# Front steps over one channel block of two tiles (4096 elements an instruction) in a fused VQ codec kernel, with engine queues found anew

## The chip, the cores and the metric

The kernel runs on one core of one Trainium2 chip. The metric is the device time of one execution in microseconds (us). Five engines of the core work side by side: TensorE (PE: matrix products, with PEld for its weight loads), VectorE (DVE), ScalarE (ACT), GpSimd (POOL) and SyncE (SP), which here does nothing but issue DMAs. Each engine works through its own queue in order.

## The reference, cut to what matters

```python
xp = pad(x, 1 row on both sides)            # x (2, 16000, 512) bf16
z = sum(xp[:, i:i+T, :] * dw_enc[i] for i in range(3))   # per-channel taps
z = silu(z)
res, q = z, 0
for s in range(4):                           # residual quantisation, codebooks (4, 8, 512)
    d2 = |res|^2 - 2 res.cb[s] + |cb[s]|^2
    sel = cb[s][d2.argmin(-1)]
    q, res = q + sel, res - sel
y = sum(qp[:, i:i+T, :] * dw_dec[i] for i in range(3))   # qp: q padded
```

So each of the 32,000 tokens is filtered along time by a three-tap filter with one weight per channel and tap, gated, assigned a code word in each of four stages, and the sum of the four chosen code words is filtered again.

## The kernel before, in words

**Tiles.** The tokens are cut into 18 tiles of G rows of 128 tokens, 9 for each batch row: G = 8, 10, 12, 16 six times | 16 six times, 12, 10, 8. Tiles 3 to 14 have G = 16, that is 2048 tokens. A tile's data lie in SBUF with channels on the partitions, four channel blocks of 128 (i = 0 to 3), in the ring buffer XR (in the code XT is its view): for each block G + 2 slots of 128 tokens, the two more for the edges. XR has 108 slots, six tiles of 18. Loading tile n + 6 therefore has to wait until tile n's residual has been read for the last time, by the grams of its fourth stage.

**Steps of a tile**, with the keys that the code gives them:
- load: SP issues one transposing DMA for each slot (L631), and one for an edge slot (L643, L649) where the neighbour is another tile. Tiles 0 and 1 are loaded otherwise (L601, transposed on PE and copied at L622).
- front, for one piece of the tile: three taps, each a product with a per-partition scalar, into TA, EX and in place into XR (L681 on ACT, L682 on DVE), two additions on DVE (L402), exp of the negative on ACT (L689), plus 1 (L691). front2: reciprocal on ACT (L700) and the gate, a product on DVE (L402). The helper `either` lets a tap, a copy or a cast run on ACT or on DVE.
- select: the grams of the first stage on PE (score0, L719), a chain of short DVE instructions (decide, L754 to L859) with transposes on PE between, by which the codes of the first three stages are chosen.
- resid: PE forms the residual behind three stages (L914, L919), ACT or DVE casts it into XR (L941, L942). score3 (L719 again) and decide (L956 on) choose the last code.
- windows and back: the one-hot codes are laid out (L878, L884, L885) and the decoder's products are made on PE (L997), cast into one of four buffers YB (L1006 on ACT, L1007 on DVE) and stored by SP (L1034).

**Pieces.** In a tile of G = 16 a piece is two channel blocks, nb = 2: exp, plus 1, reciprocal, gate and additions handle 2 x 2048 = 4096 elements per partition. A tap can't, since its scalar differs from channel block to channel block: each piece has six taps of 2048 elements. There are 36 pieces, put into groups (RUNS) of 2, 3, 3, then 4, at the end 2; the exps of a group follow each other under one table load, and so do its reciprocals. NE = 4 buffers EX hold the pieces of a group. EARLY = 2 is the number of tiles loaded the other way.

**Order.** The order of every engine's instructions is fixed by hand-written tables: RANK gives a step's place, WHERE the engine (A or D) of each step that has the choice. A planner reads them; at run time nothing but semaphores is left. The fills (L1062) are products without use that fill gaps on PE.

## Time and profile before

| | us |
|---|---|
| time of the runs shown | 579.2 and 581.91, median 580.56 |
| the profiled execution's own time | 584.83 |
| its span | 582.9 |
| DVE busy | 540.3 (93%) |
| ACT busy | 537.5 (92%) |
| PE busy | 463.2 (79%) |
| POOL busy | 80.2 (14%) |

The span is the part of the profiled execution between its first and last instruction; 584.83 − 582.9 = 1.93 us lie around it. Its own time is 584.83 − 580.56 = 4.27 us above the median of the runs. The profile lists for each engine its busy time and instructions, groups them by line, operation and shape with the mean duration of one, and names for each idle stretch what ended it. Durations of neighbouring instructions on DVE and ACT overlap a little, so what an instruction costs in a full queue is read from start to start.

### The profile page before, as it was taken

How to read it: one execution, taken by the hardware profiler on the slowest of the kernel's cores; microseconds unless marked ns; L12 is line 12 of the kernel's file. 1: busy time of each engine (PE TensorE's matmuls, PEld its weight loads, DVE VectorE, ACT ScalarE, POOL GpSimd, SP SyncE). 2: the span in 40 equal slices, each digit the busy share in tenths (PEclk: the TensorE clock that was granted, in tenths of full speed). 3: DMA queues.
4: the chain of work that ended last, by engine and by line, in shares of the span. 5: the costliest groups of instructions: out<-in, count | busy, mean ns of one | idle time of the engine just before them, and what ended most of it. 6: DMA issues, size and time to landing. Idle time of an engine off the chain costs nothing.

```text
span 582.9 us, 27362 instructions
## 1 busy us (share of the span) xinstructions
PE 463.2 (79%) x12366; PEld 226.0 (39%) x12462; DVE 540.3 (93%) x1028; ACT 537.5 (92%) x423; POOL 80.2 (14%) x140
## 2 busy tenths in 40 slices
PE   7855768768786788878886898677888888889994
PEld 4322334433433243443434244333334444445442
DVE  4999999998999899999999999999999999988642
ACT  4898999999999999999999999989999999999563
POOL 6014101002001420012000103202022112000000
PEclk9768879997899799899999899999999989999999
DMA  8444454544574555867767696696695531232354
GB/s 249 97 100 101 94 98 87 92 66 109 87 150 99 118 113 112 198 87 144 130 131 138 120 146 136 130 178 148 114 213 87 174 92 42 75 111 76 133 197 157
DMA packets 153384, 71.81 MB, mean 123 GB/s; under 512 B 144710, under 2 KB 144742, under 8 KB 153012
## 3 DMA queue, kind: packets, MB, share of 16 engines
q1 hardware_dynamic: 153052, 69.64, 56.2%
q8 instruction: 97, 1.59, 1.2%
q10 hardware_dynamic: 216, 0.43, 0.2%
q14 instruction: 19, 0.16, 0.1%
HBM read 2.79 MB, written 32.77 MB: 61 GB/s over the span
## 4 chain that ended last, share of the span: by engine, by line
DVE 31%; ACT 22%; SPq 19%; PE 15%; issue 7%; DMA 3%; DVEq 0%; ACTq 0%
SPq L631 16%; DVE XR L402 8%; ACT XR L941 5%; ACT EX L700 5%; PE banks L914 5%; ACT YB L1006 5%; DVE EX L402 4%; ACT EX L689 3%; PE banks L919 3%; DMA out_dram<-YB 3%; PE banks L719 2%; PE banks L997 2%; DVE TA L682 2%; DVE XR L682 2%; ACT EX L681 2%
## 5 line engine op out<-in xcount | busy, mean ns | idle before, releaser
L402 DVE TENSOR_TENSOR XR<-XR,EX 128x4096 bf16<-128x4096 bf16 (+3 forms) x72 | 145.0, 2020 | 0.3 <-ACT EX L700 0.2
L941 ACT CAST XR<-banks 128x1024 bf16<-128x1024 f32 (+2 forms) x125 | 110.6, 943 | 13.6 <-PE banks L919 13.5
L1006 ACT CAST YB<-banks 128x1024 bf16<-128x1024 f32 x114 | 112.9, 1048 | 9.0 <-DVE OHALL L402 2.5
L689 ACT ACTIVATE EX<-XR 128x4096 bf16<-128x4096 bf16 (+3 forms) x36 | 115.5, 3209 | 4.6 <-DVE XR L402 4.5
L700 ACT ACTIVATE EX<-EX 128x4096 bf16<-128x4096 bf16 (+3 forms) x36 | 115.4, 3212 | 0.1
L719 PE MATMUL banks<-XR 128*32 128x64 bf16 x8064 | 93.1, 201 | 14.0 <-issue 5.6
L719 PEld LDWEIGHTS <-XR 128*32 128x32 bf16 x8064 | 78.3, 98 | 58.9 <-issue 49.7
L802 POOL COPY OHDS<-OHALL 128x256 bf16<-128x256 bf16 (+3 forms) x36 | 48.4, 1344 | 361.0 <-DVE OHALL L402 346.5
L919 PE MATMUL banks<-OHR,WR 32*128 32x512 bf16 (+2 forms) x1152 | 82.9, 358 | 1.3 <-DVE OHR L859 0.7
L402 DVE TENSOR_TENSOR EX<-TA,EX 128x4096 bf16<-128x4096 bf16 (+3 forms) x36 | 72.5, 2014 | 0.0
L914 PE MATMUL banks<-XR,IDENT 64*64 64x512 bf16 (+2 forms) x576 | 56.6, 379 | 11.6 <-ACT XR L941 3.9
L1062 PE MATMUL banks<-MSK,IDENT 128*128 128x512 bf16 x200 | 58.3, 434 | 8.3 <-issue 2.9
L997 PE MATMUL banks<-WDEC,OHW 128*128 128x512 bf16 x145 | 48.6, 392 | 15.3 <-ACT XR L941 4.8
L914 PE MATMUL banks<-XR,UP 64*64 64x512 bf16 (+2 forms) x576 | 55.1, 363 | 1.5 <-issue 1.5
L919 PEld LDWEIGHTS <-WR 32*128 32x128 bf16 x1152 | 24.0, 92 | 61.2 <-issue 55.2
L682 DVE TENSOR_SCALAR TA<-XR,WENC 128x2048 bf16<-128x2048 bf16 (+3 forms) x69 | 47.2, 690 | 0.2
L914 PE MATMUL banks<-XR,DOWN 64*64 64x512 bf16 (+2 forms) x576 | 42.0, 367 | 0.0
L682 DVE TENSOR_SCALAR EX<-XR,WENC 128x2048 bf16<-128x2048 bf16 (+3 forms) x60 | 40.4, 683 | 0.7 <-DMA XR<-in_x_dram 0.6
L691 DVE TENSOR_SCALAR EX<-EX 128x4096 bf16<-128x4096 bf16 (+3 forms) x36 | 39.3, 1100 | 0.0
L682 DVE TENSOR_SCALAR XR<-XR,WENC 128x2048 bf16<-128x2048 bf16 (+3 forms) x57 | 38.4, 678 | 0.0
L1062 PEld LDWEIGHTS <-IDENT 128*128 128x128 bf16 x223 | 22.9, 108 | 34.8 <-issue 17.6
L914 PEld LDWEIGHTS <-IDENT 64*64 64x64 bf16 x576 | 19.8, 106 | 36.1 <-issue 29.1
(138 smaller groups left out, 586.2 us busy)
## 6 DMA issues: line engine op xcount, KB each, us to landing
out_dram<-YB SPq DMA_DIRECT2D x34, 448.0 KB
out_dram<-YB SPq DMA_DIRECT2D x28, 512.0 KB
XR<-in_x_dram SPq DMA_TRANSPOSE x263
out_dram<-YB SPq DMA_DIRECT2D x28, 60.0 KB
XR<-in_x_dram SPq DMA_DIRECT2D x1, 1280.0 KB
XR<-in_x_dram SPq DMA_DIRECT2D x1, 1024.0 KB
out_dram<-YB SPq DMA_DIRECT2D x30, 2.0 KB
out_dram<-YB SPq DMA_DIRECT2D x2, 224.0 KB
```

The lines of the kernel that those rows point to most:

```text
L402: add("DVE", cost, key, lambda: nc.vector.tensor_tensor(out=out, in0=a, in1=b, op=op), reads, writes, **kw)
L631: nc.sync.dma_start_transpose(out=X[:, :, g + 1, :], in_=src[g])
L682: lambda dst=to, src=src, w=w: nc.vector.tensor_scalar(out=dst, in0=src, scalar1=w, scalar2=None, op0=ALU.mult),
L689: add("ACT", act(nb * R), ("exp", n, i0), lambda: nc.scalar.activation(v(ex), Z, ACT.Exp, scale=-1.0), zt, ext + ["ACTTAB"], hold="E")
L700: nc.scalar.add_instruction(mybir.InstActivation(name=nc.get_next_instruction_name(), engine=mybir.EngineType.Activation, func=ACT.Reciprocal,
L719: nc.tensor.matmul(o[HB * q:HB * (q + 1), u * ZW:(u + 1) * ZW].rearrange("p (s c) -> p s c", s=2), lhsT=blk, rhs=both, start=False, stop=( ...
L914: nc.tensor.matmul(at(r)[to], lhsT=dia[h, h], rhs=Z[h, i, r:G:RG, :], start=start, stop=False)
L919: nc.tensor.matmul(at(r), lhsT=WR[v][g, i * P:(i + 1) * P], rhs=W[g, v // 3, 0:rows_of[r], :], start=False, stop=stop)
L941: either({"ACT": act_psum(2 * k * P), "DVE": dve(2 * k * P)}, key(1), lambda dst=dst, src=src: nc.scalar.copy(dst, src()), lambda dst=dst, ...
L997: nc.tensor.matmul(o, lhsT=W[:, k, PADC:PADC + P], rhs=WDEC[u], start=True, stop=not wrap)
L1006: either({"ACT": act_psum(1024), "DVE": dve(1024)}, key, lambda dst=dst, box=box: nc.scalar.copy(dst, ps(box)), lambda dst=dst, box=box: n ...
L1062: nc.tensor.matmul(PS[j // 2][:, 512 * (j % 2):512 * (j % 2) + NMK * ZW], lhsT=IDENT, rhs=MSK.rearrange("p u w -> p (u w)"), start=True, s ...
```

## The change

Ten of the twelve large tiles are taken in pairs, TWINS = (4,5), (6,7), (8,9), (10,11), (12,13). For these a piece is one channel block of both tiles instead of two channel blocks of one. The number of pieces stays 36, their size 4096 elements, and a tap needs one scalar now, so that it is one instruction of 4096 elements, in two runs of 2048 since the tiles lie apart in XR (`rows_from`). A piece of a pair needs both tiles' loads, and either tile's first grams need all four gates of the pair. PAIRS, an unused way of selecting two tiles at once, is taken out. RANK and WHERE are new from end to end.

```diff
+    TWINS = [(4, 5), (6, 7), (8, 9), (10, 11), (12, 13)]
-    PAIRS = ()
-    RANK = ("000304000m02000a0d050f04030109010106050d0d0g0g0q080f06040f0c0i020e0307010G0c130t0E090H0n0r0h0u000I0i10080f0k0o0w0D0O0U04"
...
+    RANK = ("000000000309040b0c01090a07020605010a0e0308020b0f070e0504000701090d0g0F0106070N0g0J0w0S080d0x1b0j0H0r0y0h0l0p0t0E0P0T0U04"
...
-    pieces = [(st, i) for st in tiles for i in range(0, KT, st["nb"])]
+    twin = {a: (tiles[a], tiles[b]) for a, b in TWINS}
+    pieces = []
+    for st in tiles:
+        if st["n"] in twin:
+            pieces += [(twin[st["n"]], i) for i in range(KT)]
+        elif not any(st in t for t in twin.values()):
+            pieces += [(st, i) for i in range(0, KT, st["nb"])]
...
+    def front_twins(sts, i):
+        G = sts[0]["G"]
+        R = G * P
+        lo, hi = sorted(st["xo"] for st in sts)
...
+        def rows_from(k):
+            one = XT[:, i, lo + k:lo + k + G, :]
+            return bass.AP(tensor=one.tensor, offset=one.offset, ap=[one.ap[0], ((hi - lo) * P, 2), (1, R)])
+        both = lambda t: t[:, 0:2 * R].rearrange("p (u x) -> p u x", u=2)
+        Z = rows_from(2)
...
+        for k, dst, tok in ((0, both(TA), [("TA", c) for c in range(KT)]), (1, both(ex), ext), (2, Z, xi)):
+            src, w = rows_from(k), WENC[:, k, i:i + 1]
+            either({"ACT": act(size) + 0.09, "DVE": dve(size, 3.84) + 0.06}, key, lambda dst=dst, src=src, w=w: nc.scalar.mul(dst, src, w),
+                   lambda dst=dst, src=src, w=w: nc.vector.tensor_scalar(out=dst, in0=src, scalar1=w, scalar2=None, op0=ALU.mult),
+                   allx + ["WENC"] + ([] if k == 2 else xi), tok)
```

The changed instruction lists differ in these counts (taps of 1024 to 1536 elements are those of the small tiles; "copies" are OHR, pads and windows from PSUM):

| | before | after |
|---|---|---|
| DVE: all rows | 1030 | 993 |
| DVE: taps of 2048 | 124 | 19 |
| DVE: taps of 4096 | 0 | 49 |
| DVE: casts into XR of 1024 / 768 / 512 | 7 / 7 / 5 | 9 / 6 / 10 |
| DVE: casts into YB | 12 | 15 |
| DVE: copies of OHR 1024 / 768 / 512, of pads 1024 | 6 / 2 / 0, 4 | 10 / 1 / 2, 7 |
| ACT: all rows | 428 | 405 |
| ACT: taps of 2048 | 20 | 5 |
| ACT: taps of 4096 | 0 | 11 |
| ACT: casts into XR of 1024 / 768 / 512 | 89 / 17 / 19 | 87 / 18 / 14 |
| ACT: casts into YB | 114 | 111 |
| ACT: copies of OHR 1024, of pads 1024 | 6, 5 | 2, 2 |
| ACT: table loads | 22 | 22 |
| SP: transposing loads, stores | 263, 132 | 263, 132 |

Where the instructions now stand is seen best at two places. In the lists below, the last number or product is the shape of the output, and a trailing x3 means three in a row.

DVE, the first taps of tile 4, before. EX, TA and XR are the taps' targets, L402 additions and decide steps, L754, L755 and L780 decide steps of earlier tiles:

```order
L691 TENSOR_SCALAR EX3_77<-EX3_77 128x4096
L682 TENSOR_SCALAR EX0_74<-XR_72,WENC_62 128x2048
L682 TENSOR_SCALAR TA_73<-XR_72,WENC_62 128x2048
L402 TENSOR_TENSOR PR_89<-PR_89,TR_92 128x80
L682 TENSOR_SCALAR TA_73<-XR_72,WENC_62 128x2048
L402 TENSOR_TENSOR KEY0_82<-PR_89,CCB_71 128x80
L754 TENSOR_REDUCE E2_91<-banks_99 128x8
L755 TENSOR_TENSOR SC_88<-banks_99,CC2_70 128x192
L780 TENSOR_REDUCE MN_93<-KEY0_82 128x10
```

DVE, the first taps of the pair (4,5), after:

```order
L793 TENSOR_REDUCE E2_91<-banks_99 128x8
L794 TENSOR_TENSOR SC_88<-banks_99,CC2_70 128x192
L689 TENSOR_SCALAR TA_73<-XR_72,WENC_62 128x4096
L689 TENSOR_SCALAR EX0_74<-XR_72,WENC_62 128x4096
L689 TENSOR_SCALAR EX1_75<-XR_72,WENC_62 128x4096
L407 TENSOR_TENSOR EX0_74<-TA_73,EX0_74 128x4096
L689 TENSOR_SCALAR TA_73<-XR_72,WENC_62 128x4096
L793 TENSOR_REDUCE E2_91<-banks_99 128x8
```

Three taps of 2048 with decide steps between have become taps of 4096 elements that stand together; three products of two different pieces follow each other.

SP, the stretch that ends with the last load that the first taps of tile 13 need (the last of the six in the last row), before. L631 are loads, L1034 stores:

```order
L631 DMA_TRANSPOSE XR_72<-in_x_dram 128x4x128 x2
L1034 DMA out_0_dram<-YB0_84 1x1024
L1034 DMA out_0_dram<-YB0_84 112x2048
L1034 DMA out_0_dram<-YB0_84 15x2048
L631 DMA_TRANSPOSE XR_72<-in_x_dram 128x4x128 x4
L1034 DMA out_0_dram<-YB2_86 128x2048
L631 DMA_TRANSPOSE XR_72<-in_x_dram 128x4x128 x6
```

SP, the stretch that ends with the last load that the first taps of the pair (12,13) need (the third of the four in the last row), after. L636 and L654 are loads, L1073 stores:

```order
L1073 DMA out_0_dram<-YB1_85 128x2048
L636 DMA_TRANSPOSE XR_72<-in_x_dram 128x4x128 x3
L654 DMA_TRANSPOSE XR_72<-in_x_dram 128x4x128
L636 DMA_TRANSPOSE XR_72<-in_x_dram 128x4x128 x15
L654 DMA_TRANSPOSE XR_72<-in_x_dram 128x4x128
L636 DMA_TRANSPOSE XR_72<-in_x_dram 128x4x128 x4
L1073 DMA out_0_dram<-YB2_86 128x2048
L636 DMA_TRANSPOSE XR_72<-in_x_dram 128x4x128 x4
```

Before, at most 14 loads stand between two stores once the first store has gone out; here there are 24 in a row ahead of one store. Counted from the start of the list, the pair's last load is the 211th and has 38 stores ahead of it; before, tile 13's last load is the 210th and has 46.

More of the change, by code (lines that the diff above doesn't have):

```diff
@@ L1042 @@
         for st, i in group:
[L1043 to L1045 removed]
+            if i == 0:
+                for u in st if isinstance(st, tuple) else (st,):
+                    if u["n"] >= EARLY:
+                        load(u)
+                        hold(u)
             done.append(front(st, i))
[L1047 to L1048 removed]
+        for d in done:
+            front2(*d)
         for st, i in group:
[L1050 to L1058 removed]
+            if isinstance(st, tuple):
+                ready = st if i + 1 == KT else ()
+            else:
+                ready = (st,) if i + st["nb"] == KT else ()
+            for t in ready:
+                select([t])
+                for sub in range(len(t["subs"])):
+                    resid(t, sub)
+                back(t)
     def fill(j, k):
```

129 lines of the change are left out of this document (66 added, 63 removed).

## The prediction

> **What bounds the kernel now.** I read the page's busy shares first, then the busy time by stretches, then the chain that ended last, then the groups by shape, at last single stretches of the timeline. The page, then the table by stretches (start:end, length, busy time of the engines with their instructions in brackets, granted TensorE clock, DMA share, GB/s):
>
> ```profile
> span 582.9 us, 27362 instructions
> PE 463.2 (79%) x12366; PEld 226.0 (39%) x12462; DVE 540.3 (93%) x1028; ACT 537.5 (92%) x423; POOL 80.2 (14%) x140
> DVE 31%; ACT 22%; SPq 19%; PE 15%; issue 7%; DMA 3%; DVEq 0%; ACTq 0%
> ...
> core 0: us, PE busy (x) PEld busy (x) DVE busy (x) ACT busy (x) POOL busy (x), PEclk, DMA share, GB/s
> 0.00:100.00 100.00, 71.47 (x928) 34.97 (x936) 91.76 (x169) 85.67 (x76) 22.49 (x76) 0.83 0.54 119
> 160.00:225.00 65.00, 51.04 (x1415) 23.74 (x1428) 63.38 (x114) 63.33 (x46) 13.81 (x9) 0.95 0.60 117
> 295.00:360.00 65.00, 53.51 (x1529) 25.30 (x1542) 64.73 (x113) 64.66 (x49) 8.63 (x7) 0.97 0.73 126
> 360.00:460.00 100.00, 80.40 (x2343) 38.09 (x2360) 97.25 (x183) 96.65 (x73) 16.48 (x17) 1.00 0.76 158
> 531.00:583.00 52.00, 42.19 (x1141) 20.68 (x1149) 27.41 (x73) 31.04 (x38) 1.15 (x5) 0.98 0.46 157
> ```
>
> DVE and ACT are both full from 100 us to 531 us: of the 65 us up to 360 DVE leaves 0.27 and ACT 0.34 open. At 531 DVE ends its last gate; after it neither is full, and PE has the most to do (42.2 of 52 us). So the time is: start, the work that DVE and ACT must do up to the last gate, their waits, and a tail of 52 us. DVE's busy time before 531 is 540.3 − 27.4 = 512.9 us, its idle time 531 − 512.9 = 18.1. Two waits at the start make 7.4 of that; 10.7 lie in the middle:
>
> ```profile
> 1.49 0.28 DVE L530 TENSOR_REDUCE SMT<-IDENT 128x4 f32<-128x128 bf16 x1 [1.49 <-POOL IDENT masks.py:199]
> 8.97 1.29 DVE L622 COPY XR<-banks 128x1024 bf16<-128x1024 bf16 x2 [5.91 <-PE banks L612]
> 529.81 1.21 DVE L402 TENSOR_TENSOR XR<-XR,EX 128x2048 bf16<-128x2048 bf16 x1
> ```
>
> A third queue is near its limit, and the chain gives it 19%: SP. Two of its rows (minimum/median/maximum ns, first to last start) and the moment at which tile 13's loads are just in time:
>
> ```profile
> L631 SPq DMA_TRANSPOSE XR<-in_x_dram x234: 1188/1266/2769, 1.7 to 478.7; - x117
> SPq L631 <- PE banks L719: 13.1, 3, 6.3
> 349.57 10.34 SPq L631 DMA_TRANSPOSE XR<-in_x_dram  x6
> 361.83 1.42 DVE L682 TENSOR_SCALAR EX<-XR,WENC 128x2048 bf16<-128x2048 bf16 x2 [0.59 <-DMA XR<-in_x_dram]
> ```
>
> SP issues a load in 1.27 us at the median; the wait for the grams of the fourth stage (13.1 us) is the wait for slots in XR. Tile 13's last load ended its issue at 349.57 + 10.34 = 359.91, and DVE's first tap came 1.92 us later, having waited 0.59.
>
> **The change, part by part.** Prices. The rows by shape (count, busy us, mean ns), then four of the timeline (start, us):
>
> ```profile
> L682 DVE TENSOR_SCALAR TA<-XR,WENC 128x2048 bf16<-128x2048 bf16 x47 | 35.2, 755 | 0.2
> L682 DVE TENSOR_SCALAR XR<-XR,WENC 128x2048 bf16<-128x2048 bf16 x39 | 28.8, 741 | 0.0
> L682 DVE TENSOR_SCALAR EX<-XR,WENC 128x2048 bf16<-128x2048 bf16 x38 | 28.4, 758 | 0.6 <-DMA XR<-in_x_dram 0.6
> L691 DVE TENSOR_SCALAR EX<-EX 128x4096 bf16<-128x4096 bf16 x24 | 29.1, 1225 | 0.0
> L691 DVE TENSOR_SCALAR EX<-EX 128x2048 bf16<-128x2048 bf16 x4 | 2.7, 678 | 0.0
> L402 DVE TENSOR_TENSOR XR<-XR,EX 128x4096 bf16<-128x4096 bf16 x48 | 109.3, 2282 | 0.0
> L402 DVE TENSOR_TENSOR EX<-TA,EX 128x4096 bf16<-128x4096 bf16 x24 | 54.8, 2281 | 0.0
> L1007 DVE CAST YB<-banks 128x1024 bf16<-128x1024 f32 x12 | 14.5, 1220 | 2.0 <-PE banks L997 1.3 <-PE banks L878 0.8
> L942 DVE CAST XR<-banks 128x512 bf16<-128x512 f32 x5 | 3.4, 689 | 2.3 <-PE banks L919 2.3
> L942 DVE CAST XR<-banks 128x1024 bf16<-128x1024 f32 x7 | 8.5, 1218 | 0.4 <-PE banks L919 0.4
> L859 DVE COPY OHR<-banks 128x1024 bf16<-128x1024 bf16 x6 | 4.1, 676 | 0.0
> L941 ACT CAST XR<-banks 128x1024 bf16<-128x1024 f32 x89 | 87.2, 1044 | 2.5 <-PE banks L919 2.4
> L859 ACT COPY OHR<-banks 128x1024 bf16<-128x1024 bf16 x6 | 6.5, 1080 | 0.0
> L700 ACT ACTIVATE EX<-EX 128x4096 bf16<-128x4096 bf16 x24 | 87.6, 3648 | 0.1
> ...
> 84.71 1.21 DVE L691 TENSOR_SCALAR EX<-EX 128x4096 bf16<-128x4096 bf16 x1
> 85.85 0.74 DVE L682 TENSOR_SCALAR EX<-XR,WENC 128x2048 bf16<-128x2048 bf16 x1
> 86.51 0.74 DVE L682 TENSOR_SCALAR TA<-XR,WENC 128x2048 bf16<-128x2048 bf16 x1
> 85.38 3.90 ACT L681 ACTIVATE EX<-XR,WENC 128x2048 bf16<-128x2048 bf16 x2
> ```
>
> From start to start a tap of 2048 costs DVE 86.51 − 85.85 = 0.66 us; the mean of the three groups (752 ns), less the same 0.08 of overlap, is 0.67, which I take. A product of 4096 on DVE costs 85.85 − 84.71 = 1.14 as "plus 1"; a tap is 752 − 678 = 0.07 dearer than a plus 1 of its size, so a tap of 4096 comes to 1.21. Merging two taps saves 2 × 0.67 − 1.21 = 0.13. On ACT two taps take 3.90 − 0.1 = 3.80; one of 4096, by the reciprocal of that size (3.65 less 0.1, and 0.07 for the scalar), 3.62: it saves 0.18. No tap of two separate runs stands in the trace, but the gate and the addition into XR do run over two separate runs, and cost 2282 ns against 2281 in one piece; so I add nothing for the runs. (If one run more cost as much as one instruction, 0.13, the 49 taps would be 6.4 us dearer, the upper bound.)
>
> The Trainium skill ("Perfetto Trace Analysis", section Optimizing Scalar/DVE Operations) puts the overhead of an instruction on SBUF data at about 60 ns on DVE and 93 ns on ScalarE, and has grouping pay only for a saturated engine. By it the merged taps would save, as an estimate, 49 × 0.06 + 11 × 0.093 = 4.0 us over both engines, where the rows give 49 × 0.13 + 11 × 0.18 = 8.4; the sum by it would be 3.4 us later on DVE.
>
> DVE's work. Of 124 taps of 2048 there stay 19, and 49 of 4096 come: 19 × 0.67 + 49 × 1.21 − 124 × 0.67 = −11.1 us. Seven taps' worth of that (4.7 us) has moved to ACT, the rest, 6.4, is the merging. What ACT hands over in return is dearer: three casts into YB (3 × 1.17 = 3.5), two casts of 1024 into XR (2.3), five of 512 (5 × 0.67 = 3.3) less one of 768 (0.9): +8.3; seven copies of 1024 and smaller ones, +5.0; the small tiles' taps +0.9. All the list: +2.9. But the YB casts and eight decide steps stand behind the last gate now or before it in other numbers: summed instruction by instruction up to the last gate, the new list is 4.4 us longer, behind it 1.7 shorter. I take **+4.4**; bounds +1 (a tap of 4096 at 1.14) and +11 (a run costs like an instruction).
>
> ACT's work. Taps: 5 × 1.90 + 11 × 3.62 − 20 × 1.90 = +11.3; small taps −2.6; casts −6.5, copies −7.6. Up to the last reciprocal the list is 6.2 us shorter. That isn't gained: ACT starts the pair's taps late. Its first cast into YB now stands ahead of the first pair's tap and needs tile 0's windows, which stand behind 93 us of DVE work, at about 102 us; ACT has then done 80 us of work against 95 on its clock. So about 8 us of ACT's idle time are new, its shorter list is eaten, and both engines reach the last gate together, ACT with the last reciprocal's end about 1 us ahead of where DVE wants it. I add **+0.8** for the start (bounds 0 and 4), and DVE's sum is the one that counts.
>
> The loads. A pair's first tap waits for both tiles. Summing the new DVE list (with the rows' durations from start to start) from the last step that the releasing grams need to the first tap gives the time that SP has: for the pair (12,13), whose later tile takes tile 7's slots, 27.6 us, where the old list gave tile 13 52 us. SP needs for it 16 loads and one store: 16 × 1.46 + 0.5, landing 1.9, and the grams themselves about 3: 28.8 us. The 1.46 lies between the median row, 1.27, and the six loads quoted above, 1.72 each, with which it would be 32.9. For (10,11): 29.8 us on DVE against about 28.5 to 33. For (8,9) the slots come free before SP gets there, and SP's own queue (104 loads by 154 us, then 34 loads and 11 stores, at the same prices) is through at 211, against a first tap near 219. For (4,5) it is 101 against 106. So there are two places with a shortfall of −1 to +5 us each; I take **+3** in all, of which 1 is compensated, since a DVE that waits lets PE's results arrive (the 10.7 us in the middle are mostly that): net **+2**; bounds −5 (half of the 10.7 goes, no load is late) and +14.
>
> SP's queue: the loads and stores are as many as before, and 24 loads in a row stand ahead of one store. Stores wait longer, but four buffers YB are there and the casts around it come in the same bursts; I cost it at nothing while the loads are on time.
>
> The tail. DVE has 1.7 us less work behind the last gate, PE a little less (two backs and a residual of tile 13 to 15 earlier): **−1.2**, bounds −4 and +3. That either tile's first grams come after all four gates of a pair lies inside the middle, where other tiles' work covers it; its price is in the middle's bounds.
>
> Sum against the profiled execution: 584.83 + 4.4 + 0.8 + 2 − 1.2 = 590.8; that execution is 4.27 above the median of the runs, so 580.56 + 6.0 = **586.6 us**.
>
> **The rivals.**
> - *Loads late at every pair.* The pair's first taps stand in DVE's queue ahead of decide steps of other tiles, on which PE and ACT wait. If a load takes 1.6 to 1.7 us rather than 1.46, both loops above fall short by 4 to 5 us and (8,9) by about 3, and 13 us come: 580.56 + 4.4 + 0.8 + 13 − 1.2 = 597.6. For it: SP's share of 19%, the 0.59 us at tile 13, the 24 loads in a row. Against it: 13.1 us of SP's waits in the run before are for slots that now come free earlier for tiles 7 and 8. It passes the 2% limit of 592.2 from a shortfall of 7.6 us net.
> - *The waits shrink.* The new order might have fewer of the 10.7 us of middle waits: 580.56 + 4.4 + 0.8 − 7 − 1.2 = 577.6. For it: the merged taps give PE longer covers. Against it: DVE's cover steps between two dependent decide steps are coarser, 1.21 instead of 0.67.
> - *Half rate.* A tap over two separate runs could fall to half the speed of a contiguous one: 49 × 1.07 = 52 us more, 638. The equal prices of the two L402 rows speak against it, though these are operations of two inputs. The Trainium skill ("VectorE: DVE Perf Modes", section What auto-detection actually checks) lets a single-source operation keep its fastest mode if both sides are in SBUF with an even outermost count; two runs are even, so by it nothing is lost. No run here shows such a tap yet.
> - The change does what it says in any case: 60 merged taps stand in the lists.
>
> **How the numbers follow.** Forecast 0.56 (its own range 581 to 592), late loads 0.23 (592 to 602), shrunk waits 0.16 (571 to 581), half rate 0.03, others 0.02. About 2% is what a measurement of this kernel can tell from no change: 569 to 592.2. Faster: a fifth of the shrunk waits, 0.03. Slower: late loads, half rate, others and a tail of the forecast, 0.23 + 0.03 + 0.01 = 0.27. Same: 0.70. The range 575 to 600 leaves out 0.05 below, 0.05 of the late loads and half rate above.
>
> **What would show it.** In the profile after: DVE rows of taps with 4096 near 1290 ns busy (1.21 + 0.08), x49, and on ACT near 3.72; DVE busy near 543, ACT near 533; ACT idle some 8 us before its first cast into YB near 100 us; DVE's waits for in_x_dram at first taps of pairs of 0 to 5 us; the last gate at about 537 us on a run like the one profiled. The prediction is wrong if the taps of 4096 cost over 1.3 from start to start, if the load waits sum to over 8 us, or if middle waits of DVE fall below 5 us.

## The result and the profile after

The changed kernel takes 602.3 us (median of 2 runs, 602.05 to 602.55) against 580.56 us: 1.0375 times the time before, with an interval of 1.0269 to 1.048. It is slower by 21.7 us, where 6 had been forecast. The profiled execution of the changed kernel took 602.55 us, that of the kernel before 584.83; between these two, whose traces are compared below, the difference is 17.7 us. The other 4 us are what the profiled execution of before lay above its median.

The page of the changed kernel, its span, its busy shares and the shares of the chain that ended last:

```profile
span 600.4 us, 27379 instructions
...
PE 484.5 (81%) x12460; PEld 231.8 (39%) x12460; DVE 547.1 (91%) x991; ACT 534.4 (89%) x400; POOL 72.9 (12%) x140
...
DVE 56%; PE 18%; ACT 9%; issue 8%; DMA 4%; SPq 3%; ACTq 0%; DVEq 0%
```

SP's share has gone from 19% to 3%: the loads are not what holds the new kernel. DVE is busy for 6.8 us more, ACT for 3.1 less. The same stretches as before, and the one from 100 to 160 us (columns as in the prediction's table):

```profile
0.00:100.00 100.00, 70.46 (x930) 34.23 (x934) 86.71 (x166) 76.40 (x70) 21.40 (x76) 0.78 0.54 119
100.00:160.00 60.00, 44.95 (x1131) 21.43 (x1124) 54.84 (x89) 49.40 (x30) 4.65 (x7) 0.80 0.50 90
160.00:225.00 65.00, 51.10 (x1192) 22.58 (x1195) 63.34 (x94) 63.05 (x37) 12.02 (x8) 0.92 0.54 109
295.00:360.00 65.00, 51.13 (x1358) 24.31 (x1351) 60.89 (x99) 60.75 (x34) 6.74 (x6) 0.95 0.60 124
360.00:460.00 100.00, 84.13 (x2491) 40.25 (x2490) 98.74 (x167) 99.04 (x74) 10.47 (x8) 0.98 0.67 143
549.00:600.40 51.40, 43.89 (x1177) 21.08 (x1169) 24.94 (x77) 30.82 (x39) 1.42 (x6) 0.96 0.43 149
```

Up to 100 us DVE and ACT have done 5 and 9 us less than before. From 100 to 160 us ACT is open for 10.6 us and DVE for 5.2, and from 295 to 360, where before a third of a microsecond was open on either, it is 4. The last gate:

```profile
547.46 1.21 DVE L407 TENSOR_TENSOR XR<-XR,EX 128x2048 bf16<-128x2048 bf16 x1
```

It ends at 548.7 us instead of 531.0; behind it lie 51.7 us instead of 51.9. So all of the loss stands ahead of the last gate. DVE's idle time up to there is 26.8 us (18.1 before), its busy time 521.8 (512.9). ACT's idle time is 45.4 (24.5), its busy time 503.3 (506.5). Since busy and idle time of either engine add up to the same moment, the two engines' losses can be read together: 8.7 + 8.9 + 20.9 − 3.2 = 35.3, half of it is 17.7, the delay of the last gate. That is the form of the table further down.

The taps, by shape:

```profile
L689 DVE TENSOR_SCALAR TA<-XR,WENC 128x4096 bf16<-128x4096 bf16 x19 | 24.5, 1292 | 0.0
L689 DVE TENSOR_SCALAR XR<-XR,WENC 128x4096 bf16<-128x4096 bf16 x15 | 19.2, 1284 | 2.0 <-PE banks L758 2.0
L689 DVE TENSOR_SCALAR EX<-XR,WENC 128x4096 bf16<-128x4096 bf16 x15 | 19.1, 1283 | 0.1
L688 ACT ACTIVATE EX<-XR,WENC 128x4096 bf16<-128x4096 bf16 x5 | 18.9, 3775 | 0.0
L688 ACT ACTIVATE XR<-XR,WENC 128x4096 bf16<-128x4096 bf16 x5 | 18.6, 3727 | 0.7 <-PE banks L758 0.7
```

The prices are those forecast (1290 ns and 3.72 us). But the taps that write into XR wait for something that no tap waited for before: grams (L758). DVE's waits of this kind, beside the one at the start that grew from 5.9 us:

```profile
DVE XR L627 <- PE banks L617: 10.5, 1, 10.5
...
DVE XR L407 <- issue: 3.9, 1, 3.9
...
DVE XR L689 <- PE banks L758: 2.0, 2, 1.5
...
DVE XR L407 <- PE banks L758: 0.9, 2, 0.5
```

The 3.9 us stand against "issue", the profile's name for a wait to which it finds no releaser. The timeline around it shows what goes on, on three engines (start, duration, in brackets the idle time before):

```profile
117.44 0.30 PE L758 MATMUL banks<-XR 128*32 128x64 bf16 x16 [0.71 <-issue]
...
117.69 3.71 ACT L688 ACTIVATE XR<-XR,WENC 128x4096 bf16<-128x4096 bf16 x1 [0.38 <-PE banks L758]
...
121.45 0.68 PE L758 MATMUL banks<-XR 128*32 128x64 bf16 x63 [3.26 <-ACT XR L688]
...
126.48 0.70 PE L758 MATMUL banks<-XR 128*32 128x64 bf16 x64
127.22 2.29 DVE L407 TENSOR_TENSOR XR<-XR,EX 128x4096 bf16<-128x4096 bf16 x1 [3.92 <-issue]
```

ACT writes a tap of the pair (4,5) into XR after grams have ended, the next grams wait 3.26 us for that tap, and the pair's addition on DVE begins when the last of these grams has ended. The grams belong to tile 1. They and the pair share no element: the tiles' slots in XR lie apart. The semaphores of the built programs say the same: in the kernel before no tap or addition waits for a gram of another tile and no gram for a tap; in the changed one 13 do (10 on DVE, 3 on ACT), and 9 grams wait for taps or additions of a pair. Where such a wait is found, both sides are patterns of two runs: the pair's writes (`rows_from`) go to two tiles' slots, the gram's second operand (`both` in the code of the grams) takes a slot and the code words at the end of XR's row. The reading that fits is that what lies between the two runs is taken as touched. It isn't a rule for every two runs: the additions and gates of the kernel before go to two runs as well, one in each of two channel blocks, and none of them waits.

At the start:

```profile
9.89 4.28 PE L617 MATMUL banks<-IDENT,XR 128*128 128x128 bf16 x48 [2.59 <-DMA XR<-in_x_dram]
...
12.67 2.48 DVE L627 COPY XR<-banks 128x1024 bf16<-128x1024 bf16 x4 [10.48 <-PE banks L617]
```

Before, DVE's first copy of pads began at 8.97 us. The new list has a first group of tile 1, which lands later, transposed on PE ahead of tile 0.

### The profile page after: what moved, and what is told of

Read it like the earlier page. It is cut to its first block, busy times and chain, and to the rows that moved or that the text cites. A ratio compares the mean times of both kernels' runs of the same rounds, so it can differ in the third digit from the quotient of the medians.

```text
span 600.4 us, 27379 instructions
## 1 busy us (share of the span) xinstructions
PE 484.5 (81%) x12460; PEld 231.8 (39%) x12460; DVE 547.1 (91%) x991; ACT 534.4 (89%) x400; POOL 72.9 (12%) x140
## 4 chain that ended last, share of the span: by engine, by line
DVE 56%; PE 18%; ACT 9%; issue 8%; DMA 4%; SPq 3%; ACTq 0%; DVEq 0%
DVE XR L407 14%; DVE EX L407 7%; PE banks L953 5%; PE banks L758 4%; ACT YB L1045 3%; PE banks L958 3%; PE banks L1036 3%; DVE XR L689 2%; DVE EX L721 2%; DMA XR<-in_x_dram 2%; DVE PR L407 2%; SPq L636 2%; DVE TA L721 2%; DVE EX L695 2%; DVE TA L689 2%
## 5 line engine op out<-in xcount | busy, mean ns | idle before, releaser
L980 ACT CAST XR<-banks 128x1024 bf16<-128x1024 f32 (+2 forms) x119 | 106.1, 943 | 22.8 <-PE banks L958 19.7
L1045 ACT CAST YB<-banks 128x1024 bf16<-128x1024 f32 x111 | 109.4, 1054 | 12.1 <-PE banks L1036 10.0
L758 PE MATMUL banks<-XR 128*32 128x64 bf16 x8064 | 93.2, 199 | 22.3 <-issue 6.9
L758 PEld LDWEIGHTS <-XR 128*32 128x32 bf16 x8064 | 77.4, 96 | 65.7 <-issue 54.9
L841 POOL COPY OHDS<-OHALL 128x256 bf16<-128x256 bf16 (+3 forms) x36 | 38.8, 1079 | 408.3 <-DVE OHALL L407 380.8
L693 ACT ACTIVATE EX<-XR 128x4096 bf16<-128x4096 bf16 x20 | 72.8, 3638 | 1.7 <-DVE XR L407 1.7
L1036 PE MATMUL banks<-WDEC,OHW 128*128 128x512 bf16 x190 | 60.4, 396 | 15.0 <-ACT XR L980 7.0
L1103 PE MATMUL banks<-MSK,IDENT 128*128 128x512 bf16 x221 | 67.3, 448 | 5.9 <-DVE PR L996 2.4
L728 ACT ACTIVATE EX<-XR 128x2048 bf16<-128x2048 bf16 (+3 forms) x16 | 42.3, 2655 | 3.4 <-DVE XR L407 2.3
L751 PE MATMUL banks<-MSK,IDENT 128*128 128x512 bf16 (+2 forms) x68 | 25.7, 378 | 6.5 <-DVE RC L809 2.4
L1036 PEld LDWEIGHTS <-OHW 128*128 128x128 bf16 x190 | 15.8, 100 | 27.3 <-issue 17.7
L981 DVE CAST XR<-banks 128x512 bf16<-128x512 f32 (+2 forms) x25 | 23.4, 942 | 2.0 <-PE banks L958 2.0
```

Source lines behind the costliest of these rows:

```text
L693: add("ACT", act(size), ("exp", n, f), lambda: nc.scalar.activation(both(ex), Z, ACT.Exp, scale=-1.0), zt, ext + ["ACTTAB"], hold="E")
L728: add("ACT", act(nb * R), ("exp", n, i0), lambda: nc.scalar.activation(v(ex), Z, ACT.Exp, scale=-1.0), zt, ext + ["ACTTAB"], hold="E")
L758: nc.tensor.matmul(o[HB * q:HB * (q + 1), u * ZW:(u + 1) * ZW].rearrange("p (s c) -> p s c", s=2), lhsT=blk, rhs=both, start=False, stop=( ...
L841: add("POOL", 1.5, key(4.2), lambda s=s, two=two, b=b, GT=GT: nc.gpsimd.tensor_copy(OHD[b][:, 0, 0:GT, 2 * s:2 * s + 2, :], two), [("OHA", ...
L980: either({"ACT": act_psum(2 * k * P), "DVE": dve(2 * k * P)}, key(1), lambda dst=dst, src=src: nc.scalar.copy(dst, src()), lambda dst=dst, ...
L1036: nc.tensor.matmul(o, lhsT=W[:, k, PADC:PADC + P], rhs=WDEC[u], start=True, stop=not wrap)
```

## The experiments

The table holds all runs beside the two kernels: the ratio to the kernel before, run beside it, with its interval, the moment of the last gate, and idle and busy time of DVE and ACT up to there, in us, from the profiled executions.

| kernel | ratio | last gate | DVE idle, busy | ACT idle, busy |
|---|---|---|---|---|
| before | 1 | 531.0 | 18.1, 512.9 | 24.5, 506.5 |
| after | 1.0375 [1.0269, 1.048] | 548.7 | 26.8, 521.8 | 45.4, 503.3 |
| ctl_03 | 1.0018 [0.9985, 1.0051] | 527.7 | 14.7, 513.0 | 22.0, 505.7 |
| ctl_12 | 0.9894 [0.9848, 0.9939] | 523.6 | 13.0, 510.6 | 17.2, 506.4 |
| pair_refound | 1.031 [1.0243, 1.0378] | 544.9 | 25.4, 519.6 | 39.4, 505.5 |
| a_exact | 1.0266 [1.024, 1.0291] | 542.0 | 17.9, 524.1 | 38.3, 503.7 |
| a_exact_split | 1.0325 [1.0301, 1.0349] | 545.2 | 16.8, 528.5 | 40.0, 505.2 |
| a_front | 1.023 [1.0194, 1.0266] | 541.9 | 20.6, 521.4 | 39.0, 502.9 |
| a_front_cover | 1.0897 [1.0853, 1.0941] | 579.6 | 60.2, 519.4 | 74.5, 505.1 |
| gates_late | 1.017 [1.0092, 1.0247] | 541.7 | 22.2, 519.5 | 28.8, 512.8 |
| gates_late_b | 1.0354 [1.0291, 1.0417] | 549.1 | 28.3, 520.9 | 34.9, 514.2 |
| start_b | 1.0489 [1.0459, 1.0519] | 553.3 | 31.8, 521.5 | 47.6, 505.8 |
| start_exact | 1.0273 [1.0231, 1.0316] | 543.7 | 20.0, 523.7 | 37.0, 506.7 |
| unpair45 | 1.0663 [1.0616, 1.071] | 561.8 | 45.6, 516.3 | 49.9, 511.9 |
| only45_x | 1.0293 [1.0245, 1.0341] | 544.4 | 30.2, 514.2 | 43.4, 501.0 |
| unpair45_x | 1.026 [1.0211, 1.0309] | 547.6 | 21.7, 525.9 | 32.7, 514.9 |
| late2_x | 1.0203 [1.0159, 1.0246] | 544.9 | 21.4, 523.6 | 31.4, 513.6 |

**The waits for grams of other tiles: a_exact and a_front.** The first writes the pair's third tap and addition, whose target is XR, one instruction per tile; list, order and engines stay.

```diff
-            either({...}, key, lambda dst=dst, src=src, w=w: nc.scalar.mul(dst, src, w), ...
-        tt(Z, Z, both(ex), ALU.add, dve(size, 1.92), key, ext + xi, zt)
+        def each(fn, *v):
+            for u in range(2):
+                fn(*[alone(w, u) for w in v])
+            run = each if k == 2 else lambda fn, *v: fn(*v)
+        add("DVE", dve(size, 1.92), key, lambda: each(lambda z, e: nc.vector.tensor_tensor(out=z, in0=z, in1=e, op=ALU.add), Z, both(ex)), ext + xi, zt)
```

> The third taps and the additions into XR of the pairs, 3 + 1 instructions of 4096 elements in two runs, are written as one instruction for each tile; all else stays. Theory (the pairs' writes in two runs are taken to collide with the grams' operand, which reaches from a slot to the code words at the row's end): DVE's waits for PE L758 before additions and taps (2.0 + 0.9) and the unnamed 3.9 us near 123 us go, PE's 3.26 us before a gram near 118 us goes; 15 third taps on DVE cost 0.13 and 20 additions 0.06 us more, 3.2 in all. Net about -3.6: 598.7 us, ratio to before about 1.031. Rival (the pair must wait for PE's real work there): the waits stay under another name, and the 3.2 us are added: 605 us.

Measured: 596.03 us (594.95 to 596.42). In the built program the waits between the pairs' writes and other tiles' grams are all gone. DVE's idle time fell by 8.9 us, ACT's by 7.1, and the time by 6, although 20 taps and 20 additions are no longer merged.

a_front leaves everything merged and moves the code words from the end of XR's row to its start.

```diff
-    XT = XR[:, :, 0:SLOTS * P].rearrange("p i (g c) -> p i g c", c=P)
+    XT = XR[:, :, 2 * NC:].rearrange("p i (g c) -> p i g c", c=P)
...
-                    both = bass.AP(tensor=blk.tensor, offset=blk.offset, ap=[blk.ap[0], (cb - at, 2), (1, HB)])
+                    both = bass.AP(tensor=code.tensor, offset=code.offset, ap=[code.ap[0], (at - cb, 2), (1, HB)])
```

> The changed kernel with all its merged taps and additions, but the words that stand at the end of a row of XR moved to the row's start, so that the range which the second operand of a gram spans is another one. In the built program 4 taps and additions wait for grams of other tiles instead of 13 (the kernel before: none). Theory (these waits are what the merged writes cost, and merging third taps and additions saves 2 to 3 us by itself): 594 to 597 us. Rival (a_exact gained because PE could begin after the first tile's write): 600 to 603 us.

Measured: 595.86 us (595.83 to 596.54). The rows of DVE's and PE's waits that are left, the second and the third of the kind:

```profile
DVE XR L407 <- ACT EX L739: 0.7, 2, 0.4
...
DVE XR L689 <- PE banks L759: 0.7, 1, 0.7
...
PE banks L759 <- DVE XR L689: 4.3, 3, 2.0
```

The second row is what remains of 6.8 us (3.9 + 2.0 + 0.9). The range between the gram's two runs matters, as supposed: with another place for 2 × NC words per row the same products, equally merged, take some 6 us less, so shorter writes as in a_exact aren't needed for it. Not all is gone, though: in the built program 4 taps still wait for grams of other tiles, and 9 grams for taps or additions of pairs with which they share no element, as many as in the changed kernel; in a_exact there are none of either. The third row, 4.3 us of PE's idle time, is grams that wait for such taps.

**What merging is worth: a_exact_split.** As a_exact, and the other two taps of a pair one instruction per tile as well, so that nothing is merged and only list and order are new: 34 more instructions on DVE and 6 on ACT.

```diff
-            run = each if k == 2 else lambda fn, *v: fn(*v)
+            run = each
```

> As a_exact, and the other two taps of each pair's piece are one instruction for each tile as well, so that nothing is merged any more but the order is the new one. Theory (DVE is full, so a merged tap saves its 0.13 us): 34 x 0.13 = 4.4 us more than a_exact on DVE, and 6 x 0.18 on ACT: 603.1 us. Rival (the taps fill time in which DVE would wait anyway): as a_exact within 1 us.

Measured: 599.35 us (598.8 to 599.74), 3.3 more than a_exact. DVE's busy time grew by 4.4 us, which is the 34 × 0.13 = 4.4 of the prediction's rows, ACT's by 1.5. The Trainium skill ("Perfetto Trace Analysis", section Optimizing Scalar/DVE Operations) would give 34 × 0.06 = 2.0 on DVE, as an estimate; the trace sides with the rows of the kernel before. So merging gives what it promised, and without it the new list takes 18 us more than the kernel before with the same taps, casts and gates, some on another engine: up to the last gate DVE's casts and copies come to 46.9 us instead of 30.6, its decide and setup steps to 129.4 instead of 124.7, its taps to 109.0 instead of 112.7, and ACT idles 15.5 us more.

**Is it the list or the pairs: ctl_03, ctl_12, pair_refound.** A list found anew might cost by itself. The two controls are the kernel before, without pairs, with other lists; the third keeps a_front's pairs and takes another list.

```diff
-    RANK = ("000304000m02000a0d050f04030109010106050d0d0g0g0q080f06040f0c0i020e0307010G0c130t0E090H0n0r0h0u000I0i10080f0k0o0w0D0O0U04"
...
+    RANK = ("...")   # another order, and another WHERE
```

> The kernel before, every tile a step of its own, no pairs; only its order is another: the list was shuffled at random and then searched anew in the same way as the spliced lists of the runs before, and DVE and ACT share the work as that search left it. Theory (a list found anew costs what the changed kernel's costs, with pairs or without): 593 to 600 us, 2% to 3% above the kernel before, with DVE and ACT idle for 10 us more each before the last gate. Rival (the pairs cost, the list's being another costs nothing): 579 to 586 us.

> As ctl_03, a second list found from another random start. Theory (a new list costs by itself): 593 to 600 us. Rival (the pairs cost): 579 to 588 us. If the two controls differ by over 5 us from each other, the luck of a list is as large as what is sought, and the share of the pairs stays open.

> a_front (pairs, all merged, words at the row's start) with another list, shuffled and searched as for the two controls. Theory (the pairs cost whatever the list): 590 to 598 us. Rival (the changed kernel's list was an unlucky one): 577 to 586 us.

Measured: 582.44 us (579.56 to 586.35), 576.85 (573.77 to 578.2) and 599.73 (599.4 to 603.16). Lists without pairs reach the time before, one of them is 1.1% faster than it; the kernels with pairs in which the XR writes or the code words are changed lie 2.3% to 3.1% above it, with the changed kernel's list (a_exact, a_front) and with another (pair_refound). So a new list doesn't cost by itself, and all lists with pairs that were tried lie above these two and the kernel before. How much the pairs cost is less sure: the two controls differ by 5.6 us, and 5 us had been set beforehand as the mark from which the luck of a list is as large as what is sought and the pairs' share stays open. The page of ctl_12:

```profile
span 574.9 us, 27390 instructions
...
PE 453.1 (79%) x12364; PEld 225.3 (39%) x12465; DVE 536.7 (93%) x1026; ACT 537.7 (94%) x425; POOL 96.7 (17%) x140
```

It is the fastest kernel of this study: the same operations as before in another order, 94% of ACT and 93% of DVE.

**Gates of both before grams of either: gates_late, gates_late_b.** Meant as one of the two bindings of a pair, put alone into the kernel before: nothing merged, every tile its own pieces, but PE's queue may take the first grams of a paired tile only behind the gates of both, and (which the change doesn't ask for) the first tile's only behind the start of the second tile's. The lists were searched as for the controls; the edit is another RANK and WHERE, here in words.

```diff
+    rule of the search, for (a, b) in (4, 5), (6, 7), (8, 9), (10, 11), (12, 13):
+        first grams of a behind the first grams of b, and both behind all gates of a and of b
```

> The kernel before, every tile a piece of its own and nothing merged, with a list searched as for the two controls but under one more rule: for the tiles that the change pairs, PE's queue holds the first grams of the one tile behind those of the other, and both behind all gates of both. Theory (grams of both tiles come late and together, so that PE and then the decide steps get their work in bunches: this binding is most of the price of a pair): 590 to 597 us. Rival (the price is that of the common loads and of coarse pieces): 576 to 584 us, as the controls. In between, 584 to 590, it is a part.

> As gates_late, a second list found under the same rule: the same numbers. If the two differ by more than 5 us, the luck of the list is as large as the effect.

Measured: 592.49 us (590.67 to 594.34) and 602.99 (602.34 to 603.85), 9 and 20 us above the kernel before. Both are slower than either control, so this rule costs; the two differ by 10.5 us, so how much it costs can't be said from two lists. Nor is it the binding as the changed kernel has it. There, too, the first grams of both tiles stand behind all four gates, but the second tile's come about as long after the first tile's as they did before the change. DVE reads the first scores of tiles 4 and 5 at these moments in the kernels before, after and gates_late:

```profile
151.43 0.41 DVE L754 TENSOR_REDUCE E<-banks 128x8 f32<-128x256 f32 x1
185.82 0.41 DVE L754 TENSOR_REDUCE E<-banks 128x8 f32<-128x256 f32 x1
```
```profile
180.39 0.42 DVE L793 TENSOR_REDUCE E<-banks 128x8 f32<-128x256 f32 x1
205.74 0.41 DVE L793 TENSOR_REDUCE E<-banks 128x8 f32<-128x256 f32 x1
```
```profile
171.61 0.41 DVE L754 TENSOR_REDUCE E<-banks 128x8 f32<-128x256 f32 x1
176.55 0.41 DVE L754 TENSOR_REDUCE E<-banks 128x8 f32<-128x256 f32 x1
```

They are 34, 25 and 5 us apart. Over the five pairs it is 17 to 34 us before, 18 to 28 after, and from −5 to 17 in the two lists of the rule, where PE's queue starts the second tile first and the grams of both come in one bunch. So what the late gates cost in the changed kernel isn't measured by these runs. Where the time goes under the rule is seen in the groups of gates_late and of ctl_12. First taps on ACT and casts on DVE, then ACT's waits for residual products, of ctl_12:

```profile
L681 ACT ACTIVATE XR<-XR,WENC 128x2048 bf16<-128x2048 bf16 (+3 forms) x12 | 21.7, 1810 | 1.0 <-DVE TA L682 1.0
L942 DVE CAST XR<-banks 128x1024 bf16<-128x1024 f32 (+2 forms) x20 | 20.6, 1032 | 3.9 <-PE banks L919 3.8
L681 ACT ACTIVATE EX<-XR,WENC 128x2048 bf16<-128x2048 bf16 x8 | 16.1, 2024 | 0.0
L1007 DVE CAST YB<-banks 128x1024 bf16<-128x1024 f32 x11 | 13.4, 1219 | 0.7 <-PE banks L997 0.7
L681 ACT ACTIVATE TA<-XR,WENC 128x2048 bf16<-128x2048 bf16 (+2 forms) x7 | 12.9, 1837 | 0.4 <-DVE EX L402 0.4
```
```profile
ACT XR L941 <- PE banks L919: 7.9, 10, 1.8
```

The same of gates_late:

```profile
L942 DVE CAST XR<-banks 128x1024 bf16<-128x1024 f32 (+2 forms) x26 | 26.2, 1013 | 3.6 <-PE banks L919 3.6
L681 ACT ACTIVATE EX<-XR,WENC 128x2048 bf16<-128x2048 bf16 (+3 forms) x14 | 25.7, 1844 | 1.1 <-DVE XR L402 1.1
L681 ACT ACTIVATE TA<-XR,WENC 128x2048 bf16<-128x2048 bf16 (+2 forms) x11 | 20.1, 1828 | 0.7 <-DVE EX L402 0.7
L1007 DVE CAST YB<-banks 128x1024 bf16<-128x1024 f32 x16 | 19.5, 1217 | 1.6 <-PE banks L854 0.5 <-PE banks L1001 0.3 <-PE banks L997 0.3
L681 ACT ACTIVATE XR<-XR,WENC 128x2048 bf16<-128x2048 bf16 (+2 forms) x11 | 19.1, 1747 | 0.1
```
```profile
ACT XR L941 <- PE banks L919: 16.4, 21, 2.2
```

ACT does 64.9 us of taps instead of 50.7, DVE 45.7 us of casts instead of 34.0. A tap of 2048 costs 1.90 us on ACT and 0.67 on DVE, a cast of 1024 costs 1.22 on DVE and 1.05 on ACT: each stands where it is dearer. A reading for these two lists, which no run tests by itself, is that the grams, decide steps and casts of two tiles come in one bunch after a stretch in which only front work was to be had, so that either engine takes what there is. ACT's waits for residual products are twice those of ctl_12, but the kernel before has 13.5 us of them too.

**DVE's exposed decide steps: a_front_cover.** DVE's decide steps (0.28 us long with 128 elements) follow each other at 0.20 us unless a step reads what the one just ahead wrote. In the changed kernel, from the timeline of DVE:

```profile
223.88 0.28 DVE L407 TENSOR_TENSOR PR<-PR,TR 128x128 bf16<-128x128 bf16 x1
224.20 0.31 DVE L407 TENSOR_TENSOR KEY<-PR,CCB 128x128 bf16<-128x128 bf16 x1
224.41 0.28 DVE L407 TENSOR_TENSOR OHALL<-KEY,MN 128x128 bf16<-128x128 f32 x1
224.61 0.28 DVE L819 TENSOR_REDUCE MN<-KEY 128x16 f32<-128x128 f32 x1
```

KEY reads PR and begins 0.32 us after it; OHALL and MN, which don't read what the step just ahead wrote, come 0.21 and 0.20 us after it. Over all steps of 128 elements ahead of the last gate of this trace, a dependent one begins 0.33 us behind the one ahead on average, another 0.20. Of short steps that read what the one just ahead wrote there are 28 ahead of the last gate before and 69 after, so some 41 × 0.12 = 5 us of DVE's new work (the expectation below has 37 more, at 0.309 against 0.192). The sums of the traces agree: decide and setup steps take 130.3 us of DVE up to the last gate instead of 124.7, though ten fewer stand there. The experiment puts another step between, in 52 places of DVE's queue:

```diff
 L407 TENSOR_TENSOR PR<-SC,CCF 128x64
 L806 CAST TR<-E_91 128x8
+L721 TENSOR_SCALAR EX_75<-XR,WENC 128x1536
 L407 TENSOR_TENSOR PR<-PR,TR 128x64
 L721 TENSOR_SCALAR TA<-XR,WENC 128x1536
 L407 TENSOR_TENSOR KEY_82<-PR,CCB 128x64
-L721 TENSOR_SCALAR EX_75<-XR,WENC 128x1536
```

> As a_front, but in DVE's queue a tap, gate or other step that stood up to ten places behind is moved between two dependent decide steps, in 52 places. Theory (DVE's extra work is the exposed time behind dependent decide steps, 0.309 against 0.192 us each, 37 of them more than before): 4 to 6 us less than a_front, DVE's busy time before the last gate 4 us shorter. Rival (a decide step that stands behind a tap of 1.2 us comes later, and PE and ACT wait for it): the same as a_front within 2 us, or slower, with the idle time of DVE and ACT grown by what was saved.

Measured: 634.92 us (633.36 to 636.39), 39 more than a_front. DVE's work fell by 2.0 us only, its idle time rose by 39.6, ACT's by 35.5. ACT's waits for residual products, of a_front and then of a_front_cover:

```profile
ACT XR L981 <- PE banks L959: 15.3, 16, 4.1
```
```profile
ACT XR L981 <- PE banks L959: 35.6, 28, 4.1
```

The first theory fell, and further than its rival had it: a decide step moved back by one tap is late for PE and then for ACT, again and again. In this list the exposed steps cost less than covering them in this way; a list searched with such covers wasn't tried.

**The start: start_b, start_exact.** The first 177 steps in the order of the kernel before, the rest as in the changed kernel; start_exact does it in a_exact.

```diff
-    RANK, WHERE = the changed kernel's
+    RANK, WHERE = the kernel before's for the first 177 steps, then the changed kernel's
```

> The changed kernel, but its first 177 steps (up to the first tap of tile 2, the transposes of tiles 0 and 1 among them) stand in the order of before, with the engines of before; the rest follows in the new order. Theory (4.1 us are lost at the start because PE transposes tile 1, which lands later, ahead of tile 0): DVE's first copy at 9.0 us instead of 12.7, and the end 4 us earlier: 598 us. Rival (the pair (4,5) waits for its loads, which end at 101 us, so what the start gains is lost there): 602 us.

> start_b with the writes of a_exact: the start as before, and no write into XR in two runs. start_b gained 4.8 us of DVE's idle time by 20 us and then lost 9.5 between 295 and 360 us, where PE's grams waited for the pairs' writes and DVE for the grams. Theory (that loss is the false collision again, and the start's 4 us are real): 592 us, against 596.0 of a_exact. Rival (the order that follows doesn't fit an earlier start, by other waits): 596 to 602 us.

Measured: 608.5 us (607.83 to 610.51) and 598.86 (597.85 to 600.28). In both DVE has idled 4 to 5 us less by 20 us (7.5 instead of 11.7 in start_exact), and neither is faster at the end: start_exact's ratio is a_exact's, and start_b lost more, between 295 and 360 us, where other tiles' grams wait for the pairs' taps, from the timeline of start_b:

```profile
312.18 0.21 PE L758 MATMUL banks<-XR 128*32 128x64 bf16 x4 [2.48 <-DVE XR L689]
314.56 0.93 PE L758 MATMUL banks<-XR 128*32 128x64 bf16 x55 [2.17 <-ACT XR L688]
```

In both, the wait taken away at the start comes back as waits between 20 us and the last gate; the rest of the list wasn't found for the earlier start.

**Which pair: unpair45, only45_x, unpair45_x, late2_x.** ACT idles 15.1 us between 88 and 142 us in the changed kernel, 2.0 before. The rows of its waits there name residual products (8.7 us) and a decide step (2.5), no load; the supposition was that the pair (4,5) comes late because of tile 5 and that ACT has no other front work. So it was tried without that pair, with it alone, and with the last two pairs alone. unpair45 joins the two known lists, the three with _x join them, write each tile's XR by itself as a_exact does, and search the list further.

```diff
-    TWINS = [(4, 5), (6, 7), (8, 9), (10, 11), (12, 13)]
+    TWINS = [(6, 7), (8, 9), (10, 11), (12, 13)]   (unpair45, unpair45_x)
+    TWINS = [(4, 5)]                               (only45_x)
+    TWINS = [(10, 11), (12, 13)]                   (late2_x)
```

> Pair (4,5) is taken apart: TWINS is (6,7), (8,9), (10,11), (12,13); the order is that of before up to the first tap of tile 6, and the new one from there. Theory (the start costs 4.1, the first pair's stage from 88 to 141 us 5.7 of DVE's idle time and 17 of ACT's): both go, 12 merged taps are lost (1.6): 602.3 - 9.8 + 1.6 = 594 us, less if ACT's time counts too, down to 588. Rival (each pair costs the same, and the first pair's delay turns up at (6,7)): 600 us.

> TWINS is (4,5) alone, writes as in a_exact. The order is spliced: the new one up to the first tap of tile 6, that of before from there, then improved step by step against the planner's own costs until nothing gained any more. Theory (the first pair, which leaves ACT without front work from 91 to 125 us, and the start carry most of the loss): 4 of the start and some 7 of the pair, 592 us. Rival (each pair costs the same fifth): 584 to 585 us.

> TWINS is (6,7), (8,9), (10,11), (12,13), writes as in a_exact, order spliced as in unpair45 and improved in the same way. Theory (without the first pair ACT and DVE have work from 88 to 142 us, and the start is that of before): 586 to 589 us. Rival (a pair costs the same wherever it stands, four fifths of the loss stay): 593 us or more.

> TWINS is (10,11), (12,13), writes as in a_exact; the order is that of before up to the first tap of tile 10, then the new one, improved in the same way. Theory (in the middle of the run other tiles' work covers a pair): 582 to 584 us. Rival (two fifths of the loss): 587 us or more.

Measured: 617.81 us (617.3 to 621.73), 599.86 (598.55 to 600.55), 598.77 (595.66 to 599.6) and 594.78 (593.67 to 596.12). The theory that the first pair carries the loss isn't borne out: without it ACT's idle time between 88 and 142 us falls to 3.1 us, and work of the same size takes its place (DVE and ACT 13 us more than a_exact). One, two, four or five pairs cost 2.0% to 2.9% (five: a_exact), so in these lists the price doesn't grow with their number. The traces before and after agree: DVE reads the first scores of tiles 4 and 5 29 and 20 us later than before, those of tiles 12 and 13 27 and 28 us. Since gates_late and gates_late_b differ by 10.5 us by the luck of their lists, four lists can't tell which pair costs what. unpair45 shows above all what an unsuitable list costs.

## Why the prediction was wrong

Against the profiled execution the prediction had 6.0 us; the traces have 17.5 between their spans. Term by term, up to the last gate:

- *DVE's work*, +4.4 forecast, +8.9 measured. (The parts named for the whole list add to +3.1, not +2.9, a difference that changes nothing.) The merged taps came out as priced, 1.20 us from start to start, 58.8 us for the 49, where 1.21 had been taken, and the casts and copies moved to DVE were in the sum. What the sum held too small is the decide steps: their instructions are the same, so they were costed as the same, but some 41 more of them stand directly behind the step whose result they read, and ahead of the last gate they came to 5.6 us more. The rival on shrunk waits names coarser cover; no term of the sum has it. The order showed it before the run: it is a count of neighbours in DVE's queue.
- *The start*, +0.8 forecast with bounds 0 and 4: DVE has idled 4.1 us more by 20 us, at the upper bound, because PE takes tile 1 first. The prediction looked at ACT's first cast into YB and not at the first copies. But in start_exact the time isn't had back.
- *The loads*, net +2 forecast: no tap of DVE waits for in_x_dram in the trace after, and SP has 3% of the chain. The middle still grew, 4.6 us for DVE, by another wait: 6.8 us at taps and additions of pairs for grams of other tiles. Neither the sum nor a rival has it; before a run it is seen in the semaphores of the built program. The 597.6 us of the rival "loads late" came nearer, by the wrong mechanism.
- *The tail*, −1.2 forecast, −0.2 measured.
- *ACT.* "About 8 us of ACT's idle time are new, its shorter list is eaten, and both engines reach the last gate together." The engines do reach it together, but ACT's new idle time is 20.9 us. Over the whole run its waits for residual products grew from 13.5 to 19.7 us and that for the first copies at the start from 7.7 to 12.1; a load is not among what ACT waits for.
- *Half rate* fell: a tap over two runs costs 1283 to 1292 ns. The Trainium skill ("VectorE: DVE Perf Modes", section What auto-detection actually checks) has nothing lost by an even outermost count, and this trace agrees.

To the end of the run these terms add up: 8.9 + 4.1 + 4.6 − 0.2 = 17.4 us where 4.4 + 0.8 + 2 − 1.2 = 6.0 had been forecast. So the first step that failed is the pricing of DVE's work by the shape of its instructions alone, 4.5 us too small; then the start, 3.3, and the middle, 2.6, which grew by a wait that no term held; the tail was 1.0 off. None of the three signs named as showing the prediction wrong appeared: the taps cost 1.20, no tap of DVE waited for a load, and DVE's middle waits were well over 5 us.

Behind the sum stands the sentence on the binding: that either tile's first grams come after all four gates of a pair "lies inside the middle, where other tiles' work covers it". It put the price of pairing tiles at nothing. The runs show a price: the pairs' list with nothing merged and without the waits between tiles that share nothing takes 18 us more than the kernel before, and the two controls without pairs take none. Which property of a pair costs it isn't shown. With DVE and ACT full to 0.3 us in 65 there was little idle time in which the work of other tiles could have covered anything. The prediction summed the new list's durations and took the old list's waits as a property of the kernel; they are a property of the list.

What makes up the 21.7 us, then: some 6 for the waits between tiles that share nothing (after against a_exact and a_front), −3.3 for the merged first and second taps (a_exact against a_exact_split), and 18 for the pairs with their list (a_exact_split against before), of which the luck of that list, some 5 to 10 us by the lists tried, can't be taken out. How these 18 divide between the late gates, the common loads and the changed order of front work stays open: the common loads weren't tried alone, and gates_late puts the grams of both tiles together, which the changed kernel doesn't. Open, too, is why a_front's time equals a_exact's (595.86 and 596.03 us; the ratios, 1.023 and 1.0266, have intervals that overlap), although 40 more of its instructions are merged; the 4 taps and 9 grams that still wait there would be the place to look.

## What to carry to other kernels

Merging two tiles' instructions saved 0.13 us per pair of instructions on DVE and 0.25 on ACT here, and it binds the tiles: the first grams of either wait for the gates of both. Where two engines are full to within a per cent, ask first what each consumer of the single tiles now waits for, and count in the new list how many dependent instructions have become neighbours. Before instructions over two distant runs go in, look which other instructions' patterns span the range between the runs, and write each tile by itself, or lay out constants so that as few as possible do.

## What the runs showed of the chip and the built program that was not expected

- A write that goes to two tiles' slots in one row of XR and a gram whose operand takes a slot and the row's end are made to wait for each other, though they share no element: 13 waits of taps and additions for foreign grams and 9 the other way, none after the third taps and additions were written tile by tile, 4 and 9 with the constants at the other end of the row; about 6 us.
- A DVE step of 128 elements that reads what the one directly ahead wrote begins 0.33 us behind it on average, another 0.20 us.
- In a_front's list the latency of the decide steps is worth more than their time: moving 52 steps in front of them, which saved 2 us of DVE work, cost 39 us.
- Two searches under the same rule ended 10.5 us apart on the chip, two without a rule 5.6 us apart. A single list is no measure of a restriction finer than that.
